# 240 of 256 columns per expert in a fused attention and mixture-of-experts kernel

## The chip, the cores and the metric

The kernel runs on one core of one Trainium2 chip. The metric is the device time of one execution in microseconds, lower is better. The times are medians of several executions; the profile is one execution recorded by the hardware profiler.

## The reference

Three layers follow one another. The first is a linear attention with decay over 2 batches, 8 heads, 768 tokens and head size 48; for each token t

```
state = alpha[t, :, None] * state + outer(k[t], v[t])
y[t]  = q[t] @ state
```

Its output, 1536 tokens of 384 values, goes to a mixture of 8 experts with one expert for each token:

```
logits = x @ w_gate;  expert = argmax(logits)
h = relu(x @ w1[expert]);  y = h @ w2[expert]        # 384 -> 1024 -> 384
out = softmax(logits)[expert] * y                    # zero past the capacity of 384 tokens
```

The third layer is one block for all tokens, 384 -> 2048 -> 384: h = x @ w_in, g = h * clip(h + 3, 0, 6) / 6, out = g @ w_out.

## The kernel before

The kernel has three stages, each with an order of instructions written out by hand.

Attention and routing: chunks of 128 tokens go through plain fp32 products (scores, keys, stage_b); emit_vg (L409) multiplies the values with the gate weights, 64 columns wide. As chunks become ready, the router picks each token's expert and place, and GpSimd scatters the token's row, weighted by its gate, to a buffer in memory, xdisp, with SLOT = 256 rows for each expert. The rows of the last two token tiles reach the first expert by another way: near_mm (L522) multiplies them with a matrix P that holds each token's gate at its place.

Experts: for each expert, read_x loads its 256 rows, trans_x turns them round on TensorE (L747), and split_x writes them as two parts, xhi (ScalarE) and xlo (VectorE), of a type called fp32r, which is fp32 rounded for TensorE. Every factor of a product is split like that, and a product of two numbers is made from three products: high by high, high by low, low by high. One step i of the stage is one 128-wide hidden tile of one expert, 64 steps in all. l1(i) makes nine products into h (L761), then hh (ScalarE, L766) and hl (VectorE, L767); l2(i) makes nine products into three accumulators o (L782). l1(i + 1) is issued ahead of l2(i). Weights are the stationary operand, 128x128 each time; the expert's rows are the moving operand, SLOT columns wide. In each step a new tile of expert weights is split too (split_hi on ScalarE, L262; split_lo on VectorE or GpSimd, L274), and a step of the conversion of the second block's weights is done (advance_f, with fc on VectorE, L55 to L63). After the last hidden tile of an expert its result is split into xth and xtl (L786, L787) at an offset that is read from memory, so that the experts' tokens come to lie one behind the other; the unused columns of one expert are overwritten by the next.

Second block: 2 groups of 768 tokens by 16 hidden tiles, products 384 columns wide (L863, L891), with ScalarE and VectorE between them (L867, L871, L874, gl at L877); the rows go out by scatters.

A flag is computed beside this: it is set where a decay exceeds 1, where a chunk decays too far, or where an expert has more than SLOT tokens. Where it is set, general_path computes everything again without these bounds.

Of the kernel before, what the change touches and what calls it, by code (L numbers as in the profile page):

```python
# [7 lines left out]
F32 = mybir.dt.float32  # L8
# [10 lines left out]
NP = 8          # head pairs (batch x 4)  # L19
SEQ = 768  # L20
C = 128         # chunk of tokens
NC = SEQ // C
NT = 12         # token tiles
# [3 lines left out]
FE = 8          # 128-wide hidden tiles of one expert  # L27
F2 = 16         # 128-wide hidden tiles of the second block
SLOT = 256      # rows held for one expert
NEAR_T = 10     # the tiles from here on reach the first expert on a way of their own  # L30
HW = 56         # value columns and gate columns of one head
RP = 112        # rows of a head pair: 48, 16 of padding, 48
HR = ((0, 64), (64, RP))    # rows of the two heads
GT = 768        # tokens in one group of the second block
PIECES = {0: ((0, 1), (1, 3), (3, 6)), 1: ((0, 2), (2, 6))}  # chunks that become ready together
TAIL = 3        # hidden tiles of the second block that are left to the end
OWN = 4096      # marks a token of the first expert: larger than any place


# Doubles come as pairs of words. A single has the sign, the top bit and the last 7 bits of the double's  # L40
# exponent, and the first 23 bits of its fraction. As a single, a double's upper word orders like the
# double itself: TINY and HUGE are the words of 2**-127 and of the last double below 2**128, times 2**16,
# which turns the second bit of the word's exponent into that of the result.
# [4 lines left out]
def to_single(nc, out, raw):  # L48
    """out[P, N] = the doubles of raw[P, N, 2] as singles, cut to 24 bits; below 2**-126 it gives 0 or less
    than 2**-126."""  # L50
    lo, hi = raw[:, :, 0], raw[:, :, 1]
    bits = out.bitcast(I32)
    nc.scalar.activation(out=out, in_=hi.bitcast(F32), func=ACTF.Abs, scale=65536.0)
    yield
    nc.vector.tensor_scalar(out=out, in0=out, scalar1=TINY, scalar2=HUGE, op0=ALU.max, op1=ALU.min)  # L55
    yield
    nc.vector.tensor_scalar(out=bits, in0=bits, scalar1=4, scalar2=1, op0=ALU.logical_shift_left,
                            op1=ALU.logical_shift_right)
    yield
    nc.vector.scalar_tensor_tensor(out=bits, in0=lo, scalar=29, in1=bits, op0=ALU.logical_shift_right,  # L60
                                   op1=ALU.bitwise_or)
    yield
    nc.vector.scalar_tensor_tensor(out=bits, in0=hi, scalar=-2147483648, in1=bits, op0=ALU.bitwise_and,  # L63
                                   op1=ALU.bitwise_or)
# [3 lines left out]
def tile_kernel(ctx: ExitStack, tc: tile.TileContext, qka, vtok, vT, wg64, wg, cap, consts,  # L68
# [38 lines left out]
    # of the last two tiles: values and logits  # L107
# [9 lines left out]
    def scatter(group, dst, idx, src, rows):  # L117
        # every row goes to a place of its own, so scatters need no order among themselves
        ins = nc.gpsimd.indirect_dma_start(  # L119
            out=dst, out_offset=bass.IndirectOffsetOnAxis(ap=idx, axis=0),  # L120
            in_=src, in_offset=None, bounds_check=rows - 1, oob_is_err=False)
        tc.declare_no_dep(ins.ins, group=group, reason="rows of scatters are disjoint")
        tc.add_to_no_dep_group(group, ins.ins)
        scattered.setdefault(group, []).append(ins.ins)
# [8 lines left out]
    def gating(pl, lg, o, po, cum, g, t0, n, res):  # L133
        """Of n tiles of logits: one-hot o of the expert, place po among its tokens, gate weight gt (0 past
        the capacity). The yields let other work in between."""
# [7 lines left out]
        # the first expert with the largest logit: its entry of idxrev is the largest  # L143
# [29 lines left out]
    def rows(pl, t0, n, res):  # L173
        # row of the dispatch: SLOT * expert + position, out of reach from position SLOT on
        po = pos[:, t0:t0 + n]
        rr = pl.tile([128, n], F32, tag=f"rr{n}", name="rr")
        nc.vector.scalar_tensor_tensor(out=rr, in0=po, scalar=float(SLOT), in1=res["r"][:, :, 0],
                                       op0=ALU.is_lt, op1=ALU.mult)
        di = pl.tile([128, n], I32, tag=f"di{n}", name="di", bufs=4)
        nc.vector.scalar_tensor_tensor(out=di, in0=rr, scalar=float(SLOT * NE), in1=po,  # L180
                                       op0=ALU.subtract, op1=ALU.add, reverse0=True)
        return di

    def finish(ps):
        """The last two tiles to the other experts, and where each expert's tokens go in the second block."""
# [36 lines left out]
    def read_x(e):  # L222
        t = xe_p[e % 2].tile([128, 2, DM], F32, tag="xr", name="xr")
        # SP's queue has weights behind; GpSimd's has the scatters before
        eng = nc.gpsimd if e == 1 else nc.sync
        ins = eng.dma_start(out=t, in_=xdisp[e * SLOT:(e + 1) * SLOT].rearrange("(c p) d -> p c d", p=128))
        if e < 3:
            after_scatters("disp", ins)
        xr[e] = t

    def alloc_x(e):
        xs_[e] = [xe_p[e % 2].tile([128, KD, SLOT], F32R, tag=f"x{n}", name=f"x{n}") for n in ("hi", "lo")]
# [46 lines left out]
    # ================= attention and routing =================  # L279
    with ExitStack() as actx:  # L280
# [34 lines left out]
        def load_piece(p, n):  # L315
            # a piece's columns of decays, keys and queries, and the first of the next
# [121 lines left out]
        def stage_b(p, c):  # L438
# [18 lines left out]
            # each head's scores meet the values of both; its own half is read  # L457
# [32 lines left out]
        # The first expert starts before the rows of the last two tiles come back from memory: products with  # L490
        # a matrix that holds each token's gate at its place put them among the rows of the tiles before.
# [27 lines left out]
        def near_mm(t, acc, first, last):  # L519
            xt = xc[:, t - NEAR_T].rearrange("p h e -> p (h e)")  # L520
            for kk in range(KD):
                nc.tensor.matmul(out=acc[kk], lhsT=xt[:, kk * 128:(kk + 1) * 128], rhs=near_s[t],  # L522
                                 start=first, stop=last, skip_group_check=True)
                if last:
                    split_x(0, kk, acc[kk])
# [10 lines left out]
        def warm_up(n):  # L536
            # TensorE runs at half its clock until it has been busy for a while
# [8 lines left out]
        with tc.manual_schedule():  # L546
# [56 lines left out]
            for i, (p, c) in enumerate(iters):  # L603
# [7 lines left out]
                if i == 12:  # L611
                    nc.gpsimd.tensor_scalar(out=upto, in0=ident, scalar1=float(OWN), scalar2=None, op0=ALU.mult)
                    nc.gpsimd.tensor_tensor(out=upto, in0=upto, in1=cst[:, 256:384], op=ALU.add)
                    # OWN + place; OWN - 1 past the capacity
# [65 lines left out]
    # ================= experts =================  # L680
# [37 lines left out]
    def advance_f():  # L718
        # one step of the work on the second block's weights
# [11 lines left out]
    with ExitStack() as ectx:  # L731
# [9 lines left out]
        def trans_x(e, ks):  # L741
            if 0 in ks:
                alloc_x(e)
            for kk in ks:
# [4 lines left out]
                split_x(e, kk, ps[:, 0:SLOT])  # L749
# [3 lines left out]
        def l1(i):  # L753
# [5 lines left out]
            for a, b in ((wh, xh), (wh, xl), (wl, xh)):  # L759
                for kk in range(KD):  # L760
                    nc.tensor.matmul(out=ps[:, 0:SLOT], lhsT=a[:, kk * 128:(kk + 1) * 128], rhs=b[:, kk, :],  # L761
                                     start=(n == 0), stop=(n == 8))
                    n += 1
            hh = h_p.tile([128, SLOT], F32R, tag="hh", name="hh")
            hl = h_p.tile([128, SLOT], F32R, tag="hl", name="hl")
            nc.scalar.activation(out=hh, in_=ps[:, 0:SLOT], func=ACTF.Relu)  # L766
            nc.vector.scalar_tensor_tensor(out=hl, in0=ps[:, 0:SLOT], scalar=0.0, in1=hh.bitcast(F32),  # L767
# [5 lines left out]
        def l2(i):  # L773
# [5 lines left out]
            for d in range(KD):  # L779
                c0 = 384 + d * 128  # L780
                for n, (a, b) in enumerate(((wh, hh), (wh, hl), (wl, hh))):
                    nc.tensor.matmul(out=yo[e][d][:, 0:SLOT], lhsT=a[:, c0:c0 + 128], rhs=b,  # L782
                                     start=(f == 0 and n == 0), stop=(f == FE - 1 and n == 2))
                if f == FE - 1:
                    ps, ov = yo[e][d], offv[e]
                    nc.scalar.activation(out=xth[:, d, bass.ds(ov, SLOT)], in_=ps[:, 0:SLOT], func=ACTF.Copy)  # L786
                    nc.vector.tensor_tensor(out=xtl[:, d, bass.ds(ov, SLOT)], in0=ps[:, 0:SLOT],  # L787
                                            in1=xth.bitcast(F32)[:, d, bass.ds(ov, SLOT)], op=ALU.subtract)

        offv = {}  # L790
        with tc.manual_schedule():
# [12 lines left out]
            for i in range(n):  # L804
# [21 lines left out]
                # GpSimd takes over where VectorE has more of the second block's weights to do  # L826
# [12 lines left out]
    # ================= second block, tokens in the order of the experts =================  # L839
    with ExitStack() as fctx:  # L840
# [60 lines left out]
        # ---- the steps above hold where no decay exceeds 1, chunks decay by no more than 1e-15 and  # L901
        # no expert has more than SLOT tokens; the flag says that one of these fails
# [7 lines left out]
        def check():  # L910
# [6 lines left out]
            # 1 where all is well  # L917
            nc.vector.tensor_scalar(out=a[:, 3:4], in0=a[:, 2:3], scalar1=float(SLOT), scalar2=None, op0=ALU.is_le)
# [12 lines left out]
        with tc.manual_schedule():  # L931
            seq = [(g, f) for g in range(2) for f in range(F2)]
            m1(*seq[0])
            for i, (g, f) in enumerate(seq):
                if i + 1 < len(seq):
                    m1(*seq[i + 1])
                # the last ones tile by tile, so that the rows go out while others are at work
# [20 lines left out]
def general_path(tc, nc, gating, ident, cst, capf, b3, qka, vT, wg, wpack, fpack, out, before):  # L958
    """The same computation for any decays and any load of the experts, with no thought of speed."""
    vr = vT.rearrange("k p t -> (k p) t")  # L960
    GN = 512
    with ExitStack() as ctx:
# [8 lines left out]
        # attention: the state of each (key, value) column by a scan over all tokens  # L971
        with tc.tile_pool(name="g_a", bufs=1) as a_p, tc.tile_pool(name="g_aps", bufs=1, space=PSUM) as aps:
# [29 lines left out]
            # gating of all tokens at once  # L1002
# [55 lines left out]
        # experts: every token by every expert, weighted by its gate  # L1058
# [10 lines left out]
        # second block  # L1069
# [91 lines left out]
```

## Time and profile before

| | |
|---|---|
| time, median of 3 runs | 504.25 us (502.42 to 505.02) |
| span of the profiled execution | 501.6 us |
| mean granted TensorE clock | 0.948 |
| TensorE busy | 460.5 us (92%) |
| weight loads busy | 438.6 us (87%) |
| VectorE busy | 332.7 us (66%) |
| ScalarE busy | 251.4 us (50%) |
| GpSimd busy | 181.6 us (36%) |

The span runs from the first to the last instruction. The profiled execution has no time of its own beside its span; the runs' median lies 2.65 us above it. In the rows PE is TensorE's products, PEld its weight loads, DVE is VectorE, ACT ScalarE, POOL GpSimd. Products overlap, so the time from one start to the next, not the length of a record, tells what one costs. The profile writes both fp32 and fp32r operands of TensorE as f32.

### The profile page before, as it was taken

The page shows a single profiled execution, that of the slowest core. Times are in us where ns is not written, and L with a number is a line of the kernel's source. Part 1 is how long each engine was busy: PE and PEld are TensorE (multiplying, and loading weights), DVE is VectorE, ACT ScalarE, POOL GpSimd, SP SyncE. Part 2 cuts the span into 40 slices and gives each one's busy share as a digit, 9 for nine tenths or more (in the row PEclk, how much of TensorE's full clock was granted, in tenths as well). Part 3 has the DMA queues.
Part 4 walks back from the last instruction along what each step waited for, and adds up shares of the span by engine and source line. Part 5 has one row for each costly group of instructions (what it writes and reads, how often), then busy time and mean ns, then how long its engine had stood idle before and what let it go on. Part 6 is the DMA issues. An engine that isn't in the chain of part 4 may idle for free.

```text
span 501.6 us, 8487 instructions
## 1 busy us (share of the span) xinstructions
PE 460.5 (92%) x3148; PEld 438.6 (87%) x3148; DVE 332.7 (66%) x647; ACT 251.4 (50%) x573; POOL 181.6 (36%) x133
## 2 busy tenths in 40 slices
PE   7959969997796899999999999999899999999993
PEld 4758858887695899899999999888899999999993
DVE  6768998577673688888877669888833444444341
ACT  3536645775143677677677554544433433333341
POOL 3335965864457054555545501221200220000003
PEclk8987985899598999999999999999999999999998
DMA  7999892141057697677776102332100031100002
GB/s 194 273 231 294 228 327 65 47 144 64 0 139 148 170 303 246 199 251 265 268 255 219 65 29 98 125 117 75 54 1 0 34 118 57 55 1 0 3 1 101
DMA packets 27539, 66.03 MB, mean 132 GB/s; under 512 B 2896, under 2 KB 14448, under 8 KB 26816
## 3 DMA queue, kind: packets, MB, share of 16 engines
q1 hardware_dynamic: 25408, 60.26, 40.1%
q0 software_dynamic: 2080, 5.13, 2.9%
q8 instruction: 27, 0.44, 0.4%
q14 instruction: 24, 0.20, 0.1%
HBM read 57.51 MB, written 7.87 MB: 130 GB/s over the span
## 4 chain that ended last, share of the span: by engine, by line
PE 48%; issue 22%; DVE 16%; DMA 4%; ACT 4%; POOL 2%; SPq 1%; another core or an unknown queue 0%; POOLq 0%; ACTq 0%; DVEq 0%
PE o L782 13%; PE h L761 13%; PE h L863 5%; PE y L464 4%; PE o L891 4%; DVE gl L877 4%; PE s L423 3%; DMA qka<-in_qka_dram 3%; PE y L461 2%; DVE fc L60 2%; ACT gh L874 2%; POOL out_dram L119 2%; DVE A L358 2%; DVE fc L63 2%; PE u L447 1%
## 5 line engine op out<-in xcount | busy, mean ns | idle before, releaser
L877 DVE SCALAR_TENSOR_TENSOR gl<-t,gh 128x384 fp32r<-128x384 f32 x64 | 47.9, 748 | 36.2 <-ACT gh L874 35.3
L274 POOL TENSOR_TENSOR wlo<-wraw,whi 128x768 fp32r<-128x768 f32 x24 | 51.1, 2135 | 55.9 <-ACT whi L262 41.6
L262 ACT ACTIVATE whi<-wraw 128x768 fp32r<-128x768 f32 (+1 forms) x68 | 55.0, 808 | 25.7 <-PE o L782 24.0
L867 ACT ACTIVATE r<-h,b 128x384 f32<-128x384 f32 x64 | 36.6, 572 | 60.2 <-PE h L863 60.1
L871 DVE SCALAR_TENSOR_TENSOR t<-r,h 128x384 f32<-128x384 f32 x64 | 35.2, 550 | 46.6 <-ACT r L867 46.5
L891 PE MATMUL o<-fh,gl 128*128 128x384 f32 x192 | 64.1, 334 | 0.0
L891 PE MATMUL o<-fh,gh 128*128 128x384 f32 x192 | 64.1, 334 | 0.0
L891 PE MATMUL o<-fl,gh 128*128 128x384 f32 x192 | 64.1, 334 | 0.0
L119 POOL DMA_INDIRECT out_dram<-o,ids x12 | 12.0, 1000 | 124.1 <-DVE o L897 120.5
L782 PE MATMUL o<-hh,whi 128*128 128x256 f32 x192 | 54.5, 284 | 2.3 <-DVE xtl L787 1.4
L274 DVE TENSOR_TENSOR wlo<-wraw,whi 128x768 fp32r<-128x768 f32 (+1 forms) x41 | 42.9, 1047 | 19.7 <-ACT whi L262 17.6
L782 PE MATMUL o<-hl,whi 128*128 128x256 f32 x192 | 54.5, 284 | 1.2 <-DVE hl L767 1.0
L782 PE MATMUL o<-hh,wlo 128*128 128x256 f32 x192 | 53.9, 281 | 0.0
L712 POOL TENSOR_TENSOR fl<-fc,fh 128x768 fp32r<-128x768 f32 x16 | 31.0, 1938 | 63.1 <-ACT fh L710 63.1
L874 ACT ACTIVATE gh<-t 128x384 fp32r<-128x384 f32 x64 | 33.4, 523 | 39.9 <-DVE t L871 39.9
L863 PE MATMUL h<-xth,fh 128*128 128x384 f32 x192 | 45.0, 341 | 4.8 <-DVE t L871 4.7
L863 PE MATMUL h<-xtl,fh 128*128 128x384 f32 x192 | 43.7, 335 | 0.0
L863 PE MATMUL h<-xth,fl 128*128 128x384 f32 x192 | 43.6, 334 | 0.0
L402 ACT ACTIVATE kh<-qka,ra 64x128 f32<-64x128 f32 x96 | 38.1, 397 | 6.8 <-POOL qka L369 3.0
L863 PEld LDWEIGHTS h<-xth,fh 128*128 128x128 f32 x192 | 33.5, 188 | 7.7 <-DVE t L871 7.0
L761 PE MATMUL h<-xhi,whi 128*128 128x256 f32 x192 | 36.6, 296 | 3.8 <-issue 3.7
L782 PEld LDWEIGHTS o<-hh,whi 128*128 128x128 f32 x192 | 36.5, 190 | 3.0 <-DVE xtl L787 1.6
(168 smaller groups left out, 1099.4 us busy)
## 6 DMA issues: line engine op xcount, KB each, us to landing
wraw<-in_wpack_dram SPq DMA_DIRECT2D x32, 768.0 KB, 4.4
fr<-in_fpack_dram SPq DMA_DIRECT2D x16, 768.0 KB, 5.5
qka<-in_qka_dram SPq DMA_DIRECT2D x6, 1011.1 KB, 12.6
xdisp<-warm SPq DMA_DIRECT2D x1, 3072.0 KB
al<-in_qka_dram SPq DMA_DIRECT2D x8, 339.1 KB, 3.0
xr<-xdisp SPq DMA_DIRECT2D x7, 384.0 KB, 4.9
vx<-in_vtok_dram SPq DMA_DIRECT2D x6, 224.0 KB, 5.2
vx<-in_vtok_dram SPq DMA_DIRECT2D x2, 672.0 KB, 19.3
```

Source lines behind the costliest of these rows:

```text
L262: nc.scalar.activation(out=w_sp[i][0][:, cols], in_=w_raw[i][:, cols], func=ACTF.Copy)
L274: eng.tensor_tensor(out=lo[:, cols], in0=w_raw[i][:, cols], in1=hi.bitcast(F32)[:, cols], op=ALU.subtract)
L402: nc.scalar.activation(out=t[r0:r1, h, :], in_=kb[p][r0:r1, c * C:(c + 1) * C], func=ACTF.Copy, scale=ra[p][r0:r1, c:c + 1])
L712: nc.gpsimd.tensor_tensor(out=lo, in0=t, in1=hi.bitcast(F32), op=ALU.subtract)
L761: nc.tensor.matmul(out=ps[:, 0:SLOT], lhsT=a[:, kk * 128:(kk + 1) * 128], rhs=b[:, kk, :], start=(n == 0), stop=(n == 8))
L782: nc.tensor.matmul(out=yo[e][d][:, 0:SLOT], lhsT=a[:, c0:c0 + 128], rhs=b, start=(f == 0 and n == 0), stop=(f == FE - 1 and n == 2))
L863: nc.tensor.matmul(out=ps[:, 0:384], lhsT=a[:, kk * 128:(kk + 1) * 128], rhs=b[:, kk, c0:c0 + 384], start=(n == 0), stop=(n == 8))
L867: nc.scalar.activation(out=r, in_=ps[:, 0:384], func=ACTF.Relu, bias=b3)
L871: nc.vector.scalar_tensor_tensor(out=t, in0=r, scalar=6.0, in1=ps[:, 0:384], op0=ALU.min, op1=ALU.mult)
L874: nc.scalar.activation(out=gh[:, sl], in_=t, func=ACTF.Copy, scale=1.0 / 6.0)
L877: nc.vector.scalar_tensor_tensor(out=gl[:, sl], in0=t, scalar=1.0 / 6.0, in1=gh.bitcast(F32)[:, sl], op0=ALU.mult, op1=ALU.subtract)
L891: nc.tensor.matmul(out=po[g][t][:, 0:DM], lhsT=a[:, t * 128:(t + 1) * 128], rhs=b[:, 384:768], start=(f == 0 and n == 0), stop=(f == F2 - ...
```

## The change

A second constant, TOK = 240, takes the place of SLOT as the number of columns that are computed for an expert: in the tiles xhi, xlo, hh and hl, in the moving operands of l1 and l2, in the splits, and in the writes of xth and xtl. The layout in memory keeps 256 rows for each expert, and the transposes and the near products keep 256 columns. The flag is now set where an expert has more than 240 tokens. The diff takes the comments out of the file as well.

```
+TOK = 240
...
-        xs_[e] = [xe_p[e % 2].tile([128, KD, SLOT], F32R, tag=f"x{n}", name=f"x{n}") for n in ("hi", "lo")]
+        xs_[e] = [xe_p[e % 2].tile([128, KD, TOK], F32R, tag=f"x{n}", name=f"x{n}") for n in ("hi", "lo")]
...
-                    split_x(0, kk, acc[kk])
+                    split_x(0, kk, acc[kk][:, 0:TOK])
...
-                split_x(e, kk, ps[:, 0:SLOT])
+                split_x(e, kk, ps[:, 0:TOK])
...
-                    nc.tensor.matmul(out=ps[:, 0:SLOT], lhsT=a[:, kk * 128:(kk + 1) * 128], rhs=b[:, kk, :],
+                    nc.tensor.matmul(out=ps[:, 0:TOK], lhsT=a[:, kk * 128:(kk + 1) * 128], rhs=b[:, kk, :],
                                      start=(n == 0), stop=(n == 8))
...
-            hh = h_p.tile([128, SLOT], F32R, tag="hh", name="hh")
-            hl = h_p.tile([128, SLOT], F32R, tag="hl", name="hl")
-            nc.scalar.activation(out=hh, in_=ps[:, 0:SLOT], func=ACTF.Relu)
-            nc.vector.scalar_tensor_tensor(out=hl, in0=ps[:, 0:SLOT], scalar=0.0, in1=hh.bitcast(F32),
+            hh = h_p.tile([128, TOK], F32R, tag="hh", name="hh")
+            hl = h_p.tile([128, TOK], F32R, tag="hl", name="hl")
+            nc.scalar.activation(out=hh, in_=ps[:, 0:TOK], func=ACTF.Relu)
+            nc.vector.scalar_tensor_tensor(out=hl, in0=ps[:, 0:TOK], scalar=0.0, in1=hh.bitcast(F32),
                                            op0=ALU.max, op1=ALU.subtract)
...
-                    nc.tensor.matmul(out=yo[e][d][:, 0:SLOT], lhsT=a[:, c0:c0 + 128], rhs=b,
+                    nc.tensor.matmul(out=yo[e][d][:, 0:TOK], lhsT=a[:, c0:c0 + 128], rhs=b,
...
-                    nc.scalar.activation(out=xth[:, d, bass.ds(ov, SLOT)], in_=ps[:, 0:SLOT], func=ACTF.Copy)
-                    nc.vector.tensor_tensor(out=xtl[:, d, bass.ds(ov, SLOT)], in0=ps[:, 0:SLOT],
-                                            in1=xth.bitcast(F32)[:, d, bass.ds(ov, SLOT)], op=ALU.subtract)
+                    nc.scalar.activation(out=xth[:, d, bass.ds(ov, TOK)], in_=ps[:, 0:TOK], func=ACTF.Copy)
+                    nc.vector.tensor_tensor(out=xtl[:, d, bass.ds(ov, TOK)], in0=ps[:, 0:TOK],
+                                            in1=xth.bitcast(F32)[:, d, bass.ds(ov, TOK)], op=ALU.subtract)
...
-            nc.vector.tensor_scalar(out=a[:, 3:4], in0=a[:, 2:3], scalar1=float(SLOT), scalar2=None, op0=ALU.is_le)
+            nc.vector.tensor_scalar(out=a[:, 3:4], in0=a[:, 2:3], scalar1=float(TOK), scalar2=None, op0=ALU.is_le)
```

## Rows read from the trace of the kernel before

**Rows 1.** Stretches: PE, PEld, DVE, ACT, POOL busy us (records), clock, DMA share, GB/s
```profile
133.00:153.00 20.00, 19.27 (x147) 18.30 (x146) 13.05 (x40) 9.65 (x19) 8.22 (x8) 0.93 0.45 118
153.00:157.00 4.00, 0.68 (x2) 0.49 (x3) 1.17 (x4) 0.57 (x2) 3.06 (x4) 0.92 0.64 26
157.00:195.00 38.00, 35.82 (x288) 35.16 (x288) 26.99 (x44) 24.15 (x46) 14.76 (x10) 0.96 0.75 219
195.00:206.00 11.00, 9.89 (x81) 9.48 (x81) 9.63 (x13) 6.98 (x14) 6.26 (x4) 1.00 0.79 279
206.00:287.00 81.00, 81.00 (x688) 80.79 (x686) 61.09 (x103) 57.69 (x109) 44.11 (x21) 1.00 0.65 220
287.00:300.00 13.00, 13.00 (x74) 12.67 (x74) 8.34 (x16) 5.99 (x12) 0.22 (x1) 1.00 0.03 6
```

**Rows 2.** The chain that ended last: start us, us, what
```profile
153.43 3.27 issue
...
199.97 2.46 DVE fc L60
...
278.29 1.06 PE o L782 x9
...
300.14 1.91 DVE gl L877
```

**Rows 3.** Groups on TensorE by shape: count, busy us, mean ns
```profile
L782 PE MATMUL o<-hl,whi 128*128 128x256 f32 x192 | 54.5, 284 | 1.2 <-DVE hl L767 1.0
...
L761 PE MATMUL h<-xlo,whi 128*128 128x256 f32 x192 | 33.8, 285 | 0.0
```

**Rows 4.** TensorE in order of time, expert stage: start us, us
```profile
222.94 0.28 PE L782 MATMUL o<-hh,whi 128*128 128x256 f32 x1
...
224.00 0.52 PE L761 MATMUL h<-xhi,whi 128*128 128x256 f32 x3
```

**Rows 5.** TensorE in order of time, second block, eleven starts
```profile
375.67 0.33 PE L891 MATMUL o<-fh,gh 128*128 128x384 f32 x1
...
377.40 0.33 PE L891 MATMUL o<-fl,gh 128*128 128x384 f32 x1
```

**Rows 6.** Weight loads in order of time, attention: start us, us, count
```profile
54.81 0.75 PEld L409 LDWEIGHTS g<-wgs,vt 128*128 128x128 f32 x6
...
55.77 0.53 PEld L464 LDWEIGHTS y<-vx,sc 128*128 128x128 f32 x4
```

**Rows 7.** Groups of weight loads by shape
```profile
L782 PEld LDWEIGHTS o<-hl,whi 128*128 128x128 f32 x192 | 36.5, 190 | 1.9 <-DVE hl L767 1.8
...
L409 PEld LDWEIGHTS g<-wgs,vt 128*128 128x128 f32 x72 | 9.1, 193 | 2.5 <-issue 2.1 <-ACT x L467 0.4
```

**Rows 8.** Groups on ScalarE and VectorE by shape
```profile
L766 ACT ACTIVATE hh<-h 128x256 fp32r<-128x256 f32 x64 | 24.5, 382 | 19.6 <-PE h L761 14.9 <-PE o L782 3.5 <-PE g L161 0.6
...
L874 ACT ACTIVATE gh<-t 128x384 fp32r<-128x384 f32 x64 | 33.4, 523 | 39.9 <-DVE t L871 39.9
...
L767 DVE SCALAR_TENSOR_TENSOR hl<-h,hh 128x256 fp32r<-128x256 f32 x64 | 26.8, 419 | 11.4 <-ACT hh L766 10.6
...
L274 DVE TENSOR_TENSOR wlo<-wraw,whi 128x384 fp32r<-128x384 f32 x2 | 1.1, 551 | 0.0
```

**Rows 9.** VectorE and TensorE in order of time, one expert step
```profile
224.56 0.41 DVE L767 SCALAR_TENSOR_TENSOR hl<-h,hh 128x256 fp32r<-128x256 f32 x1
...
225.20 0.28 PE L782 MATMUL o<-hl,whi 128*128 128x256 f32 x1
```

**Rows 10.** Plain fp32 products: groups by shape, then starts in order of time
```profile
L522 PE MATMUL s<-P,xc 128*128 128x256 f32 x8 | 3.1, 529 | 1.7 <-DVE P L516 1.7
...
L522 PE MATMUL kp<-P,xc 128*128 128x256 f32 x4 | 1.7, 506 | 0.0
...
121.30 1.04 PE L522 MATMUL s<-P,xc 128*128 128x256 f32 x4
122.18 0.59 PE L522 MATMUL kp<-P,xc 128*128 128x256 f32 x2
```

## Prediction

> **What bounds the kernel now.** I read the table of stretches first, then the chain of work that ended last, then the groups of instructions, and last the instructions in order of time, where single starts can be subtracted.
>
> The stretches [rows 1] show the expert stage from 133 to 287 us, 154 of the span's 501.6 us. The reader is to see that TensorE is the busy engine in it: 81.00 of 81.00 us from 206 to 287, with the clock granted in full (1.00, the 2.4 GHz level), while VectorE is busy 61.09 and ScalarE 57.69 of those 81 us. TensorE's idle time lies before that: 0.73, 3.32, 2.18 and 1.11 us in the four stretches ahead of it, 7.3 us in all. The chain [rows 2] agrees: it runs through h (L761) and o (L782), about 1.06 us for each nine products, and leaves TensorE only at two places worth naming, 3.27 us of "issue" at 153 us and 2.46 us of VectorE at 200 us. So a shorter product in this stage is worth its saving, nearly one for one. Behind the stage TensorE stays full until 300 us [rows 1], and from there to 361 us the chain goes through VectorE (gl, fc), whose work starts when the experts' results are there and so moves with them.
>
> **What the change does, part by part.** The products h (L761) and o (L782) are 64 hidden tiles times 9 each, 1152 in all; six groups of 192 are in the listing, two of them shown [rows 3]. All their moving operands go from 256 to 240 columns. Nothing else on TensorE changes: the transposes (L747) and the near products (L522) keep 256.
>
> *Price of a product now.* Nine start-to-start steps from 222.94 to 224.00 us are 1.06 us, 117.8 ns each [rows 4]. At 384 columns ten steps from 375.67 to 377.40 us are 1.73 us, 173 ns each [rows 5]. One column per cycle at 2.4 GHz would be 106.7 and 160 ns, so both kinds stream one column per cycle and carry 11 and 13 ns more. The line through the two points is 0.431 ns a column: 16 columns less are 6.9 ns, and 240 columns would take 110.9 ns.
>
> *What a product cannot go below.* Each product loads its own 128 columns of weights. In the attention stage, at full clock, products with only 64 moving columns (L409) load their weights six times in 0.75 us, one load lasting 0.19: (0.75 - 0.19) / 5 = 112 ns from load to load [rows 6]. With 112 moving columns (L464) four loads take 0.53 us: (0.53 - 0.19) / 3 = 113 ns [rows 6]. The moving side differs almost twofold and the pace doesn't, so 112 ns is the pace of the loads. The expert products' loads last as long, 190 ns against 193 [rows 7], so I take the same floor. Then 240 columns cost the larger of 110.9 and 112: 112 ns, 5.8 ns less than now. The lower bound is no floor at all, 6.9 ns less; the upper bound within this kind is that the present 117.8 ns is already these loads' own pace, and nothing is gained. I take 112, because the products at 384 carry the same overhead over their streaming as those at 256, which a pace of loads would not give them.
>
> The Trainium skill, "TensorE: Matmul & The Clock Gate", section "LDWEIGHTS (loading the stationary operand)", states that a load takes its number of columns divided by 1.2 GHz, 107 ns for 128. The trace's 112 ns [rows 6] agrees within 5 ns. [...]
>
> *The sum.* 1152 x 5.8 ns = 6.7 us. Off go the first seven hidden tiles (18 products each; the 147 records up to 153 us [rows 1] hold transposes and near products too), which lie ahead of the 3.27 us stall: if what ends that stall keeps its own time, their 7 x 18 x 5.8 ns = 0.7 us is only waited out. Off go also some 0.8 us, a part of the idle time that VectorE sets around 200 us [rows 2]: its conversion step (fc) lasts 2.46 us there and doesn't shorten. That leaves 5.2 us.
>
> *The other edits.* The splits hh, hl, xhi, xlo, xth and xtl have 16 columns less. hh is 382 ns at 256 columns, and a ScalarE copy of 384 is 523 [rows 8], so 16 columns are 18 ns; for hl (419 ns) and a VectorE split of 384 (551 ns) they are 16 ns. Both engines have a quarter of the dense stretch free [rows 1], and that idle time hides them, so I cost them at nothing; without that cover 64 x 16 ns would be 1.0 us, a gain. The last split of the near way goes from 256 to 240 columns too; its three pieces are the same 16 to 18 ns each. The check compares the largest count with 240 instead of 256, the same instruction. No transfer, queue or wait is added.
>
> *What is late next.* In the dense stretch hl ends at 224.56 + 0.41 = 224.97 us and its first product starts at 225.20 us [rows 9]: 0.23 us of slack. A hidden tile shortens by 18 x 5.8 = 104 ns. VectorE works 61.09 us in 81, so it isn't full and the slack renews itself, but single tiles can wait; that is in the 0.8 us above, and up to 3 us in the range.
>
> The sum stands against the profiled execution: span 501.6 us becomes 496.4. The median of the runs, 504.25 us, is 2.65 us above that span; I leave this difference as it is: 504.25 - 5.2 = 499.0 us. The likeliest case's own range is 496 to 502 us.
>
> **The rivals.**
>
> *First: narrow products leave the one-column-per-cycle regime (slower).* The trace has this type only at 256 and 384 columns; every narrower fp32 product in it is of the plain kind. A plain product appears as two records: L522 has 12 records (8 and 4) for 2 tiles x 3 parts [rows 10], while L782 has 192 for 64 x 3 [rows 3]. Each record at 256 columns takes (122.18 - 121.30) / 4 = 0.22 us [rows 10], so a plain product costs 0.44 us, near four cycles a column, where the rounded kind costs 0.118. If 240 columns fall under a size below which the rounded kind is run like the plain one, a product costs 0.44 x 240 / 256 = 0.41 us, 0.29 us more; 1152 x 0.295 = 340 us, less the 7.3 us of idle time that it would cover: 504.25 + 333 = 837 us. It decides as soon as that size lies between 240 and 256. Half the penalty (two cycles a column, 0.21 us) gives 504.25 + 1152 x 0.09 - 7 = 601 us. For it speaks that no row shows the rounded kind narrower, so the regime is unproven; against it, that between 384 and 256 the price follows the columns without a sign of a step.
>
> *Second: the loads or VectorE take it back (no change).* If the rounded kind's loads pace at 117 ns themselves, or hl becomes the last to arrive in each tile, the stage keeps its length: between 502.5 and 505 us, say 503.7. For it: TensorE's weight loads are busy 80.79 of 81 us in the dense stretch [rows 1], and hl's slack is 0.23 us. Against it: the 112 ns of rows 6, and VectorE's quarter of free time.
>
> *Third: the change sends tokens the general way.* Worked out from the reference with its default draw, the experts get 162 to 227 tokens, none above 240, so the flag stays zero. Were it set, every token would meet every expert in plain fp32, far beyond 837 us. I give it 0.01.
>
> **How the numbers follow.** The shorter product 0.42, no change 0.20, the plain regime 0.32 and its half 0.05, the general way 0.01. The first is faster by over 0.5% (2.5 us, about what a measurement of this kernel tells from no change), the second within it, the rest slower: 0.42, 0.20, 0.38. The cases of both signs hold most of the chance, and without the plain regime 0.33 would be left out; so the range goes from 496 us (no floor, the whole saving nearly kept: 504.25 - 1152 x 6.9 ns = 496.3) to that regime's 837 us.
>
> **What the changed profile would show.** Right: starts of o spaced 110 to 113 ns in the dense stretch, about 720 records in 81 us instead of 688, the last o some 5 us earlier, the second block's stretches as long as now and only shifted. The floor would show as 112 ns where the line says 110.9. Wrong: spacing near 118 ns (the loads), a wait of o on VectorE's hl in most tiles (the second rival), or products of 0.2 or 0.4 us and twice the records (the first). What would make the prediction wrong above all is that first rival: one unproven row decides between 5 us less and over 300 us more.

## The result and the profile after

The changed kernel takes 499.42 us (median of 4 runs, 498.87 to 500.06) where the kernel before takes 503.85 us (4 runs, 502.42 to 505.02): a ratio of 0.9897, with a 95% interval of 0.986 to 0.9933. The forecast was 499.0 us. In a later comparison, where the kernel before took 498.72 us, the changed one took 496.04 us, a ratio of 0.9943 (0.9914 to 0.9972). So the gain is clear of no change both times; by the medians it is 4.4 us in the first comparison and 2.7 us in the second. All ratios leave out executions more than 1.5% above the fastest of their kernel, so they can differ a little from the quotient of the medians.

The price of a product is read as in [rows 4], from the instructions of TensorE in order of time (start us, length us):

```profile
221.82 0.27 PE L783 MATMUL o<-hh,whi 128*128 128x240 f32 x1
...
222.83 0.50 PE L762 MATMUL h<-xhi,whi 128*128 128x240 f32 x3
```

Nine starts in 1.01 us, 112.2 ns each, where the kernel before had 117.8. The prediction's two candidates were 112 (the loads) and 110.9 (the straight line). The groups by shape answer to [rows 7] and [rows 8] (busy us, mean ns of one, idle time before):

```profile
L783 PEld LDWEIGHTS o<-hl,whi 128*128 128x128 f32 x192 | 36.8, 192 | 4.1 <-DVE hl L768 4.1
...
L767 ACT ACTIVATE hh<-h 128x240 fp32r<-128x240 f32 x64 | 23.6, 368 | 14.5 <-PE h L762 13.6 <-PE g L162 0.5 <-PE g L199 0.3
...
L768 DVE SCALAR_TENSOR_TENSOR hl<-h,hh 128x240 fp32r<-128x240 f32 x64 | 25.6, 401 | 10.6 <-ACT hh L767 10.0
```

A load is as long as before (192 ns against 190), hh and hl are 14 and 18 ns shorter, and the loads' idle time on VectorE's hl is 4.1 us against 1.8 [rows 7]. The chain that ended last shows where the second block begins, in the kernel before

```profile
286.86 6.75 PE h L863 x36
```

and in the changed one, with the places where it leaves TensorE on the way there:

```profile
159.46 19.21 DMA wraw<-in_wpack_dram
183.16 2.19 DVE fc L61
...
199.63 2.41 DVE fc L61
...
283.44 6.71 PE h L864 x36
```

The second block starts 3.42 us earlier, and the span is 3.3 us shorter (498.3). The products alone are worth 1152 x 5.6 ns = 6.5 us, so this execution gave some 3 us back. The stretches say where (busy us of PE, PEld, DVE, ACT, POOL with their records, then clock, DMA share, GB/s):

```profile
133.00:157.00 24.00, 23.40 (x196) 22.47 (x195) 18.11 (x51) 13.97 (x29) 12.26 (x12) 0.98 0.57 110
157.00:161.00 4.00, 4.00 (x38) 4.00 (x38) 2.00 (x4) 1.29 (x3) 3.24 (x3) 1.00 0.89 286
161.00:167.00 6.00, 0.75 (x8) 0.59 (x7) 2.06 (x3) 1.83 (x3) 0.57 (x1) 0.82 1.16 110
167.00:172.00 5.00, 5.00 (x25) 5.00 (x26) 0.90 (x3) 1.48 (x3) 0.00 (x0) 0.53 0.90 253
172.00:191.00 19.00, 17.23 (x143) 16.25 (x142) 13.96 (x21) 11.44 (x24) 8.75 (x5) 1.00 0.85 244
191.00:204.00 13.00, 11.89 (x106) 11.69 (x106) 11.24 (x18) 8.66 (x18) 6.20 (x3) 1.00 0.76 242
204.00:281.00 77.00, 76.58 (x677) 76.00 (x676) 62.12 (x102) 56.08 (x106) 44.99 (x21) 1.00 0.69 232
```

The stall that the kernel before has at 153 us comes at 161 us here, 5.25 us of idle TensorE, against 3.32 [rows 1], with the clock at 0.53 behind it. The chain then has a weight transfer of 19.21 us (159.46 to 178.67), and 1.77 us more are lost from 172 to 191 us. The waits of the stretch from 157 to 170 us name transfers as what ended the stall:

```profile
PE t L748 <- DMA xr<-xdisp: 5.2, 1, 5.2
ACT whi L263 <- DMA wraw<-in_wpack_dram: 5.0, 1, 5.0
```

TensorE's idle time is 0.60 + 5.25 + 1.77 + 1.11 + 0.42 = 9.2 us against 7.3 before [rows 1], 1.9 us of the 3. The rest, some 1.3 us, isn't the clock: the kernel before has stretches at half clock (0.50) too, and TensorE works as long in them. First the two of the kernel before, 2.85 + 3.10 = 5.95 us of products, then those of the changed one, 1.15 + 4.75 = 5.90 us:

```profile
133.00:135.90 2.90, 2.85 (x12) 2.38 (x11) 1.62 (x7) 0.95 (x3) 0.00 (x0) 0.51 0.00 0
156.30:159.80 3.50, 3.10 (x14) 3.10 (x15) 1.38 (x2) 1.19 (x2) 2.60 (x3) 0.51 0.71 64
```

```profile
133.00:134.20 1.20, 1.15 (x5) 0.78 (x3) 0.56 (x2) 0.54 (x2) 0.00 (x0) 0.51 0.00 0
164.90:171.70 6.80, 4.75 (x23) 4.78 (x24) 2.96 (x5) 2.19 (x6) 0.00 (x0) 0.50 0.90 197
```

The longer waits of the loads on hl lie in it, but no table here assigns it in full. From 204 to 281 us TensorE is busy 76.58 of 77.00 us at 113 ns a record, as forecast.

### The profile page after: what moved, and what is told of

Read it like the earlier page. It is cut to its first block, busy times and chain, and to the rows that moved or that the text cites. A ratio compares the mean times of both kernels' runs of the same rounds, so it can differ in the third digit from the quotient of the medians.

```text
span 498.3 us, 8487 instructions
## 1 busy us (share of the span) xinstructions
PE 458.0 (92%) x3148; PEld 436.2 (88%) x3148; DVE 329.7 (66%) x647; ACT 249.7 (50%) x573; POOL 175.9 (35%) x133
## 4 chain that ended last, share of the span: by engine, by line
PE 66%; DVE 15%; DMA 8%; ACT 4%; issue 3%; SPq 1%; POOLq 0%; POOL 0%; ACTq 0%; DVEq 0%
PE h L864 15%; PE o L892 14%; PE o L783 11%; PE h L762 10%; PE y L465 4%; PE s L424 4%; DMA wraw<-in_wpack_dram 4%; DVE gl L878 3%; DMA qka<-in_qka_dram 3%; PE y L462 3%; DVE fc L61 2%; DVE fc L64 2%; ACT gh L875 2%; PE u L448 2%; PE g L410 1%
## 5 line engine op out<-in xcount | busy, mean ns | idle before, releaser
L783 PE MATMUL o<-hl,whi 128*128 128x240 f32 x192 | 54.3, 283 | 2.6 <-DVE hl L768 2.4
L783 PE MATMUL o<-hh,whi 128*128 128x240 f32 x192 | 53.6, 279 | 1.0 <-ACT hh L767 1.0
L783 PE MATMUL o<-hh,wlo 128*128 128x240 f32 x192 | 53.2, 277 | 0.0
L783 PEld LDWEIGHTS o<-hl,whi 128*128 128x128 f32 x192 | 36.8, 192 | 4.1 <-DVE hl L768 4.1
L424 PE MATMUL s<-qka,kh 112*128 112x128 f32 x192 | 36.2, 319 | 4.0 <-DVE sc L427 3.3
```

The lines of the kernel that those rows point to most:

```text
L424: nc.tensor.matmul(out=s[:, h * C:(h + 1) * C], lhsT=kh[p, c][:, h, :], rhs=qh[p][:, lo:hi], start=True, stop=True)
L783: nc.tensor.matmul(out=yo[e][d][:, 0:TOK], lhsT=a[:, c0:c0 + 128], rhs=b, start=(f == 0 and n == 0), stop=(f == FE - 1 and n == 2))
```

## The experiments

The theory: the shorter products make the gain, down to a floor of 112 ns that their weight loads set; what is missing to 6.5 us is lost to the transfers' stall and to VectorE. The rivals: the shorter splits make the gain; no floor, so that narrower is better still; a narrower product leaves its one-column-per-cycle regime, only not yet at 240.

**Products alone.** The splits keep 256 columns.

```
-TOK = 240
+TOK = 256
+COLS = 240
...
+                    nw = TOK if n == 0 else COLS                  # l1
+                    nw = TOK if f == 0 and n == 0 else COLS       # l2
```

> The splits keep 256 columns; of the products, the first of each group of nine in h and of each of the 24 accumulators in o has 256 columns, the other 512 + 552 = 1064 have 240. If the products carry the gain, starts of o in the dense stretch are 112 ns apart and the time is 499.4 + 88 x 5.8 ns = 499.9 us (499 to 501). If the shorter splits carry it, the time stays at that of the kernel before, 503.9 us.

Measured: 498.69 us against 503.09 for the kernel before on the same chip, ratio 0.9945 (0.9908 to 0.9981). Nine starts of o take 1.00 us, 111 ns each:

```profile
251.68 0.27 PE L786 MATMUL o<-hh,whi 128*128 128x240 f32 x1
...
252.68 0.51 PE L764 MATMUL h<-xhi,whi 128*128 128x256 f32 x3
```

The forecast of 499.9 us would be a ratio of 0.9921 to the 503.85 us of the first comparison, inside the interval; no gain, 1, is outside. The gain is there without the shorter splits.

**Splits alone.** The products keep 256 columns; columns 240 to 255 of their moving operands are zeros in buffers that stay in place.

```
+        if e > 1:
+            xs_[e] = xs_[e - 2]
+            return
...
+            nc.gpsimd.memset(z.bitcast(F32)[:, :, TOK:COLS], 0.0)
...
+            hh, hl = hbuf[i % 3]
```

> The splits hh, hl, xhi, xlo, xth and xtl have 240 columns, all products keep 256; columns 240 to 255 of the moving operands are zeros written once, in fixed buffers. If the products carry the gain, starts are 117.8 ns apart and the time is that of the kernel before, 503.9 us (503 to 505). If the splits carry it, 499.4 us.

Measured: 515.54 us, ratio 1.0265. It tells nothing of the splits: h (L769) waited 18.7 us for GpSimd's zeros of xhi, which stood behind the scatters on that engine. With the zeros on VectorE:

> The run with short splits again, with the zeros of the fixed buffers written by VectorE instead of GpSimd, so that they don't queue behind the scatters. If the products carry the gain, starts are 117.8 ns apart and the time is that of the kernel before within 1 us. If the splits carry it, 4 us less than that.

Measured: 500.66 us against 500.15, ratio 1.0002 (0.9971 to 1.0033), with nine starts in 1.05 us, 117 ns each:

```profile
250.52 0.28 PE L789 MATMUL o<-hh,whi 128*128 128x256 f32 x1
...
251.57 0.52 PE L769 MATMUL h<-xhi,whi 128*128 128x256 f32 x3
```

The shorter splits are worth nothing that can be measured; by the interval that is less than 1.7 us either way.

**228 columns.** `TOK = 228`, still no fewer than the largest expert has.

> 228 columns instead of 240, all else as in the changed kernel. If the weight loads are the floor, starts stay 112 ns apart and the time is 499.4 us (498.5 to 500). If the price follows the columns (0.431 ns each), starts are 105.7 ns apart and the time is 499.4 - 1152 x 12 x 0.431 ns = 493.4 us.

Measured: 498.13 us against 503.09, ratio 0.9921 (0.9882 to 0.9959). The rival's 493.4 us against a kernel before of 503.85 is a ratio of 0.979, outside the interval. Nine starts take 1.00 us, 111 ns each, not 105.7:

```profile
250.31 0.28 PE L783 MATMUL o<-hh,whi 128*128 128x228 f32 x1
...
251.31 0.50 PE L762 MATMUL h<-xhi,whi 128*128 128x228 f32 x3
```

**248 columns.** `TOK = 248`, on the other side of the floor.

> 248 columns instead of 240. By the straight line between 256 and 384 columns a product takes 117.8 - 8 x 0.431 = 114.4 ns, above the floor of 112 ns, so half of the saving: starts 114 to 115 ns apart and a full hidden tile in 2.06 us instead of 2.02. If only the change from 256 to something less matters, starts are 112 ns apart.

Measured: one run, 494.42 us on a chip where the kernel before took 498.72; nine starts in 1.04 us, 115.6 ns each, between 112 and 117.8 and 1 ns above the line:

```profile
249.92 0.28 PE L783 MATMUL o<-hh,whi 128*128 128x248 f32 x1
...
250.96 0.51 PE L762 MATMUL h<-xhi,whi 128*128 128x248 f32 x3
```

So the price follows the columns down to some 240 and stays there: the floor.

**192, 160 and 128 columns.** Most products are cut further, `COLS = 192`, `COLS = 160` and `COLS = 128`, with the splits at 240. Each was run once, and the results leave out columns: these runs are for the trace alone.

> The 1064 products that are not the first of their group have 192 columns; columns 192 to 239 are left out of the sums. Load floor with the clock granted in full: 112 ns from start to start and a time within 3 us of the changed kernel. Load floor at the lower clock level: the loads' pace doubles to 213 ns with a granted clock of 0.50, as the run with 128 columns shows it, and the time is near 595 us. Four cycles a column below some width: 320 ns at a granted clock of 1.00, and over 700 us.

Measured: 495.32 us; the kernel before took 500.15 on that chip. Stretch of the run with 192 columns, then the first and the last of nine products of o:

```profile
200.00:280.00 80.00, 79.42 (x699) 78.54 (x698) 64.11 (x107) 57.93 (x110) 46.03 (x21) 1.00 0.66 225
```

```profile
221.96 0.28 PE L786 MATMUL o<-hh,whi 128*128 128x192 f32 x1
...
222.85 0.28 PE L786 MATMUL o<-hh,wlo 128*128 128x192 f32 x1
```

Eight steps in 0.89 us are 111 ns each at a clock of 1.00: a product of 192 columns costs what one of 240 costs.

> The 1064 products that are not the first of their group have 128 columns; columns 128 to 239 of the results are left out of the sums. If the loads are the floor, starts stay 112 ns apart (108 to 113) and the time stays within 3 us of 499.4 us. If the price follows the columns, starts are 62 ns apart, and VectorE and ScalarE become the bound. If the type leaves its regime somewhere below 240 columns, starts are 213 ns apart, near four cycles a column, and the time is some 600 us.

Measured: 595.87 us, 96 us above what the floor alone was expected to give. Stretches of that run:

```profile
137.00:141.00 4.00, 4.00 (x38) 4.00 (x37) 3.15 (x10) 2.34 (x5) 1.45 (x2) 1.00 0.37 108
141.00:145.00 4.00, 4.00 (x39) 4.00 (x37) 2.86 (x7) 2.26 (x4) 2.79 (x3) 1.00 0.84 287
145.00:150.00 5.00, 4.08 (x34) 3.61 (x32) 3.00 (x6) 2.11 (x5) 3.96 (x4) 1.00 0.86 135
150.00:155.00 5.00, 0.48 (x2) 0.48 (x3) 0.41 (x1) 0.72 (x2) 3.45 (x5) 0.79 0.88 62
155.00:160.00 5.00, 5.00 (x25) 5.00 (x25) 1.77 (x3) 1.36 (x4) 3.01 (x3) 0.50 0.71 198
...
160.00:350.00 190.00, 190.00 (x900) 190.00 (x899) 80.01 (x141) 79.80 (x148) 45.55 (x25) 0.50 0.45 144
```

The time alone would have looked like the regime rival. The starts tell it apart, first at a clock of 1.00, then at 0.50:

```profile
138.61 0.27 PE L786 MATMUL o<-hh,whi 128*128 128x128 f32 x1
...
139.62 0.50 PE L764 MATMUL h<-xhi,whi 128*128 128x240 f32 x3
```

```profile
259.61 0.41 PE L786 MATMUL o<-hh,whi 128*128 128x128 f32 x1
...
260.89 0.84 PE L764 MATMUL h<-xhi,whi 128*128 128x240 f32 x3
```

At a clock of 1.00 nine steps take 1.01 us, 112 ns each, where four cycles a column would take 213. Only behind the stall at 150 us, with the clock at 0.50, do six steps take 1.28 us, 213 ns each. (A short stretch can't give the pace: from 137 to 141 us 38 records overlap the 4.00 us, the ones cut by its ends among them, which would read as 105 ns; the changed kernel's 240 columns have the same 38 from 157 to 161 us.) The floor is there at either level and doubles as the clock halves.

Before the run with 160 columns it was left open whether the clock would stay or fall; 493 to 500 us were expected with it kept, near 595 us with it lost. Measured: 604.96 us. The whole expert stage of that run is at 0.50:

```profile
129.00:386.00 257.00, 253.90 (x1198) 253.35 (x1196) 104.13 (x200) 100.04 (x185) 68.05 (x44) 0.50 0.40 123
```

That the floor is the pace of the loads is read from its staying at 111 to 113 ns whatever streams past, 64 and 112 columns in the attention stage [rows 6] and 128, 192, 228 and 240 here, while each product brings a load of 128 columns. No run gave a product a narrower load or none.

**The scatters of the tokens' places moved.** The stall lies where GpSimd scatters 12 lists of token numbers (idsd) while weights are on their way. They are moved to the second block:

```
+        while not fw2_p:
+            yield
         for t in range(NT):
             scatter("ids", idsd[:, :], si[:, t:t + 1], tokid[:, t:t + 1], NT * 128)
+            yield
...
+                step(2)
```

With 240 columns:

> The changed kernel with the twelve scatters of the tokens' places, and the load that reads them back, issued in the first half of the second block instead of in hidden tiles 3 to 10 of the expert stage. If these scatters hold up the weights' transfers, the stall of 5 to 8 us in hidden tiles 8 to 14 goes, and the time falls to some 493 us with a smaller spread. If the transfers are slow there for another reason, the stall stays and so does the time, 498 to 500 us.

Measured: 491.33 us against 500.15, ratio 0.9835 (0.9795 to 0.9876). A smaller spread isn't shown: six runs lie 5.2 us apart, seventeen of the kernel before 6.2. With 256 columns:

> The kernel before (256 columns) with the same scatters moved. Without the stall in between, the distance to the run with 240 columns and late scatters should be 64 x 0.105 = 6.7 us if the loss of the changed kernel came from the stall, and stay near 4.5 us if VectorE takes a part back in every expert.

Measured: 494.14 us, ratio 0.9861 (0.9813 to 0.9909). Both are faster than the kernel before, and in these two profiles the stall is gone: from 157 to 193 us TensorE is busy 34.61 and 36.00 of 36 us. First the run with 240 columns, then the one with 256:

```profile
157.00:193.00 36.00, 34.61 (x305) 34.20 (x305) 29.58 (x47) 24.66 (x47) 15.46 (x7) 1.00 0.75 267
```

```profile
157.00:193.00 36.00, 36.00 (x308) 36.00 (x308) 28.38 (x47) 25.30 (x49) 12.19 (x6) 1.00 0.74 257
```

The weight transfers issued from 140 to 180 us land in 13.3 us (median of 7) in the changed kernel and in 4.5 us (median of 9) with 240 columns and late scatters:

```profile
wraw<-in_wpack_dram SPq DMA_DIRECT2D x7, 768.0 KB, 13.3
```

```profile
wraw<-in_wpack_dram SPq DMA_DIRECT2D x9, 768.0 KB, 4.5
```

Without the stall the expert stage can be compared by itself, from the first h to the second block. With 240 columns, the first product and the chain's piece:

```profile
132.77 1.40 PE L765 MATMUL h<-xhi,whi 128*128 128x240 f32 x3
```

```profile
272.94 6.74 PE h L867 x36
```

With 256:

```profile
134.22 1.42 PE L764 MATMUL h<-xhi,whi 128*128 128x256 f32 x3
```

```profile
279.20 6.73 PE h L866 x36
```

140.17 us against 144.98: 4.8 us shorter, of 6.5 that the products save. Of the 1.7 us that are missing, VectorE's hl takes some 1 us. The waits from 176 to 276 us have, with 240 columns,

```profile
PEld o L786 <- DVE hl L771: 2.7, 5, 1.3
PE o L786 <- DVE hl L771: 1.8, 4, 1.1
```

and with 256 columns

```profile
PEld o L785 <- DVE hl L770: 1.6, 2, 1.2
PE o L785 <- DVE hl L770: 1.0, 1, 1.0
```

That is 0.8 us more for the products and 1.1 us more for their loads; the rest of the 1.7 us isn't assigned.

The medians differ by 2.8 us only, with six runs each and intervals of 0.4 to 0.5% on either side; they neither confirm nor exclude the 4.8 us of the two profiles.

**The changed kernel and the late scatters side by side.**

> The changed kernel as it is, beside the one with late scatters on the same chip. By its profile it saves 6.7 us in the products and gives about 1.9 us back to waits on VectorE: 4.7 us under the kernel before, a ratio near 0.9905, with the stall in hidden tiles 8 to 14 in both.

> 240 columns and late scatters, beside the changed kernel on the same chip: 8 us under it, near 491 us, if the stall costs 8 us in most executions; 3 us or less under it if the stall was only in the profiled ones.

Measured: 496.04 us (0.9943, 0.9914 to 0.9972) and 489.98 us (0.9815, 0.9765 to 0.9864), with the kernel before at 498.72. The late scatters bring 6 us more than the changed kernel, between the two cases expected. In two comparisons on two chips they are 8.8 and 8.7 us under the kernel before, so the gain isn't a thing of the profiled executions alone. The changed kernel's ratio missed: the expected 0.9905 lies below its interval. And not every stall goes with these scatters: the profile of this run with late scatters, its longest execution (495.94 us, the others 486.36 to 490.97), has 3.60 us of idle TensorE at 149 us, at the transposes of an expert's rows, whose load GpSimd issued at 148.87 us where in the earlier run it was 143.06; the changed kernel's profile beside it, its longest execution too (505.21 us), has 3.86 us there:

```profile
PE t L751 <- DMA xr<-xdisp: 3.6, 1, 3.6
```

## Why the prediction was right

**What bounds the stage** held: products alone gave the gain, splits alone none (1.0002).

**The price of a product** held: 112.2 ns against the 112 taken, with the floor where the plain products of the attention stage had shown it [rows 6]. That it is the loads and not the straight line's 110.9 could not be told from 240 columns; 228, 192 and 128 columns showed it, at 111 to 112 ns. The Trainium skill, "TensorE: Matmul & The Clock Gate", section "LDWEIGHTS (loading the stationary operand)", gives the number of columns divided by 1.2 GHz, 107 ns for such a load; the run with 128 columns shows 112 ns from start to start at a clock of 1.00 and 213 at 0.50, so by these runs the figure is near the pace at the full clock.

**The sum**, 5.2 us, was measured as 4.4 us by the medians first, 2.7 us in the second comparison and 3.3 us in the profile. That the forecast time lies 0.4 us from the first measured one is in part luck: it stood on a median of 504.25 us, the kernel before came out at 503.85 us beside it, and the second comparison gave half of the sum. The saving of 6.7 was 6.5. The 0.8 us for VectorE had about the right size: where the stall is out of the way, hl costs 0.8 to 1.1 us more than with 256 columns, and it is the wait that the prediction named, with its 0.23 us of slack. The term that was too small is the stall. The prediction took 0.7 us, the head start that would be waited out. In the profiled execution the stall came 8 us later, lasted 5.25 us instead of 3.32, and behind it a second late transfer cost more. Its place isn't fixed by the program: it begins 19 us behind the first h with 228 columns and 27 us behind it with 248. One execution's distance should not be costed to tenths.

**The other edits** at nothing: right, the splits are 14 to 18 ns shorter, hidden.

**The rivals.** The plain regime doesn't exist at 240, 228 or 192 columns, and at 128 columns the 112 ns at full clock exclude it as well; that range went as high as 837 us for a case that no row of the trace spoke for beyond its absence. The second rival, loads at 117 ns themselves, fell too; its other half, VectorE, took 0.8 to 1.1 us of 6.5. That no token went the general way is shown by the time alone, 499.42 us where it was put far beyond 837.

**Where the stall comes from.** That moving the scatters of idsd takes some 6 us off is shown, with 240 columns and with 256, and two of the three profiles have no stall left. Why transfers of 768 KB and of 384 KB take up to 19 and 15 us beside scatters of 4 bytes a token was not tried; the move also frees GpSimd in the expert stage, and the runs don't separate the two.

## What to carry to other kernels

In these runs a product with a weight load of its own costs the larger of two things: its streaming with some 11 to 13 ns on top (173 ns at 384 columns, 117.8 at 256) and a floor of some 112 ns, both at the full clock. Look in the same trace for products that are narrower still: their pace from start to start is the floor, and cutting columns pays down to it and no further. Before a stage is made faster, take the waits out of it that keep their own time: here moving twelve small scatters to a later stage brought 6 us, the narrower products 2.7 to 4.4. And when a cut makes a kernel slower than arithmetic allows, read the granted clock of the stretch before believing in a new regime.

## What the runs showed of the hardware that was not expected

With 128 columns TensorE kept the full clock (1.00) from 133 to 150 us, lost it in a stall of 5 us, and did not get it back in 190 us in which it was busy 190.00 us. It was back at 1.00 from 382 us on, when the second block with its products of 384 columns had begun. With 160 columns the clock was at 0.50 already when the stage began, stayed there through 257 us in which TensorE was busy 253.90, and rose at 391 us, again when the second block had begun. In the changed kernel, with 240 columns, the clock fell to 0.50 behind a stall of the same length and was at 1.00 again from 172 us on. So a TensorE that the profile shows busy throughout may still be at the lower of its two levels. The two runs at half clock took 595.87 and 604.96 us, the one with 192 columns 495.32.
